# Weight copies spread out, splits without a table, two units' scores moved

## The chip, the cores and the metric

The kernel runs on one core of one Trainium2 chip. The metric is the device time of one execution in microseconds (us); the time before is the median of three executions. Five engines work side by side, each through its own instructions in order: PE (matrix multiply), ACT (activations and copies), DVE (vector), POOL (GpSimd) and SP, which here only issues DMAs. An instruction that waits holds up everything behind it on its engine, on SP's queue too.

## The reference, cut to what matters

```python
scores = np.matmul(q, k.transpose(0, 1, 3, 2)) / np.sqrt(D)       # q, k, v: 8 x 8 heads x 576 x 64
mask   = (rel >= 0) & (rel < 64)                                  # rel = query position - key position
attn   = softmax(np.where(mask, scores, -1e9))
x      = np.matmul(attn, v).transpose(0, 2, 1, 3).reshape(4608, 512)
h      = x @ w_in                                                 # 512 x 2048
g      = h * np.tanh(np.log1p(np.exp(h)))                         # mish; h itself above 20
out    = g @ w_out                                                # 2048 x 512
```

## The kernel before

The 4608 tokens are cut into 12 chunks of 384. A *unit* is one chunk of one pair of heads; there are 48, four to a chunk. A unit's **scores** (L433, 24 small matmuls) go through the softmax on DVE and ACT (L463 and L467, six blocks of 128 x 128; L479, L480 and L487 normalise). The result is turned: DVE transposes blocks of 32 x 32 (L525), one DMA writes the tile to DRAM (`turned`, L535), four DMAs read it back in the other order (`pT`, L533). Then PE forms the unit's **values** (L546). So between a unit's scores and its values stand ACT, DVE and five DMAs on SP.

The feed-forward part works in f32 by splitting an operand into a rounded part and a remainder, with three products for one. It has 16 blocks f of the hidden width. For chunks 0 to 3, `ffn_in` (L579) fills one of two PSUM banks `h`, ACT applies mish from the bank (L609, which frees it), the result is split (L618 to L624), and `ffn_out` (L656) adds into three banks.

Chunks 4 to 11 are taken two at a time, in four super-blocks, and for them the first matrix product is done with 7 products in place of 8 on combinations of operands. For that, `combine(i)` (L851) prepares, while chunks 2 and 3 run, seven matrices for each of the eight pairs of blocks (i, i + 8): three are plain quarters of the weights, copied SBUF to DRAM (L858), four are made by two sums (L863) and four differences (L868) on DVE, rounded on ACT (L871), the remainder formed on DVE (L872), and written to the same DRAM tensor `wc` (L875). A combine works in three tiles `o`, which also hold chunk 0 and 1's outputs until they are stored (L665). In the super-blocks `fetch` (L1036) brings one matrix after another back into seven slots.

On the other side `rebuild` (L1006) forms the seven combinations of the activations: `blend` (L1003) adds and subtracts on DVE, `split` rounds on ACT (L995, the *snap*) and forms the remainder on DVE (L996), into tiles that held weights. A blend is followed by splits that read its result, so ACT and DVE wait for each other in turn. A super-block then runs eight rounds i of seven products (L1051); the two banks X and V are read out by ACT (L1059) and DVE (`settle`, L1064).

The order on every engine is made by a list scheduler (`Plan.order`): of the tasks that are ready by its own cost table it takes the one with the lowest rank. ACT holds one table of functions at a time. A task that names a table (`exp` for the softmax, `mish`) puts a table load (L1241) in front of itself when another is in place, and is ranked 150 later for it; a task that names none runs under either. Tasks of chunks 2 and 3 stand in nine groups: within a group are some `ffn_in` blocks, then values and scores of one or two units, then the `ffn_out` of the group before. Group g of chunk 2 and 3 carries the ranks 1000 + 10 * step.

Of the kernel before, what the change touches and what calls it, by code (L numbers as in the profile page):

```python
# [9 lines left out]
F32 = mybir.dt.float32  # L10
# [198 lines left out]
def tile_window_attn_mish_ffn(  # L209
# [641 lines left out]
    def combine(i, rank):  # L851

        plan.key = None
        d, db = combined[i]
        (fa, fab), (fb, fbb), (hs, hsb) = zip(o_ring.tiles, o_ring.bufs)
        pair = i, i + NS
        for f, half, at in ((i, 0, 0), (i, 1, 1), (i + NS, 1, 2)):
            add("SP", "move", lambda f=f, half=half, at=at: nc.sync.dma_start(  # L858
                d[:, at * WP:(at + 1) * WP].rearrange("p (a n) -> p a n", a=2), ws[f][0][:, :, half * HW:(half + 1) * HW].bitcast(F32)),
                reads=[wbufs[f][0]], writes=[db], rank=4000 + i, size=P * WP * 4, after=[sums[1]])  # L860
        x = None
        for f, t, tb in ((i, fa, fab), (i + NS, fb, fbb)):
            x = add("DVE", "sum5", lambda f=f, t=t: nc.vector.tensor_tensor(  # L863
                t, ws[f][0][:, 0, :].bitcast(F32), ws[f][0][:, 1, :].bitcast(F32), ALU.add),
                reads=[wbufs[f][0]], writes=[tb], rank=rank, after=[x] if x else [])
        for o, a, b, tb in ((fa[:, :HW], fb[:, :HW], fa[:, :HW], fab), (fb[:, :HW], fb[:, HW:], fb[:, :HW], fbb),
                            (fb[:, HW:], fb[:, HW:], fa[:, :HW], fbb), (fa[:, HW:], fa[:, HW:], fb[:, HW:], fab)):
            x = add("DVE", "sub2", lambda o=o, a=a, b=b: nc.vector.tensor_tensor(o, a, b, ALU.subtract),  # L868
                    writes=[tb], rank=rank, after=[x])
        for t, tb, at in ((fa, fab, 3), (fb, fbb, 5)):  # L870
            y = add("ACT", "hi5", lambda t=t: nc.scalar.copy(hs.bitcast(F32R), t), reads=[tb], writes=[hsb], rank=rank, after=[x])  # L871
            add("DVE", "sum5", lambda t=t: nc.vector.tensor_tensor(t.bitcast(F32R), t, hs, ALU.subtract),  # L872
                reads=[hsb], writes=[tb], rank=rank, after=[y])
            for part, u, ub in ((0, hs, hsb), (1, t, tb)):
                add("SP", "move", lambda u=u, at=at, part=part: nc.sync.dma_start(  # L875
                    d[:, at * WP:(at + 2) * WP].rearrange("p (q a n) -> p q a n", q=2, a=2)[:, :, part, :],
                    u.rearrange("p (q n) -> p q n", q=2)), reads=[ub], writes=[db], rank=rank, size=P * WP * 4)
# [5 lines left out]
            groups.append([(c, f + i) for i in range(size)])  # L883
            f += size
    first = 5
    COMBINE = {0: [0], 1: [1], 2: [2], 3: [3], 4: [4], 5: [5, 6], 6: [7]}
    runs = {}

    def run(g, kind, i):
        runs.setdefault(g, []).append((kind, i))  # L890
# [4 lines left out]
    for g in range(4):  # L895
        for i in range(2):
            run(first + g, "v", 16 + 2 * g + i)
            run(first + g, "s", 18 + 2 * g + i)

    class Part:  # L900
        def __init__(self, late, k):
# [18 lines left out]
    for g, steps in enumerate(groups):  # L920
        r = 1000 + 10 * step
        for c, f in steps:
            ffn_in(c, f, 1000 + 10 * step, True, False)
            step += 1
        if g == first - 1:
            raws = [(Part(raw_late[p // 2], p % 2), [joined(xbufs[0]) for _ in range(2)]) for p in range(NPAIR)]
        asked = {kind: [units[i] for k, i in sorted(runs.get(g, [])) if k == kind] for kind in "vs"}
        near, far = H[(hs[0] + 1) % 2], H[hs[0] % 2]
        double = len(asked["v"]) > 1 or len(asked["s"]) > 1
        for _, b in (near, far) if double else ():  # L930
            assert b.readers or not b.writers
        first_v, last_v = (asked["v"][:1], asked["v"][1:]) if g < first and double else (asked["v"], [])
        for n, u in enumerate(asked["v"]):
            u.o = (near, B[1])[n] if double else B[2]
            assert u.o[1].readers or not u.o[1].writers

        def pay(vs):
            for u in vs:
                values(u, r, True)
                refill_v(u.n)  # L940

        def trailing(n):
            for c, f in held[:n]:
                ffn_out(c, f, r + 15, True)
            del held[:n]

        apart = g >= first
        if apart:
            trailing(1)
        else:  # L950
            pay(first_v)
        for n, u in enumerate(asked["s"]):
            u.place = doubled(n, near, far) if double else whole(B[:2])
            scores(u, r, True)
            refill_qk(u.n)
        pay([] if apart else last_v)
        for u in asked["s"]:
            softmax(u, 1480 if g == len(groups) - 1 else r + 20, False)
        if apart:
            trailing(1)  # L960
            pay(asked["v"])
        for u in asked["v"]:
            x_parts(u, r + 15)
        for u in asked["s"]:
            turn_dma(u, 1480 if g == len(groups) - 1 else r + 20)
        trailing(len(held))
        held = list(steps)
        for i in COMBINE.get(g, ()):
            combine(i, r + 25)
# [15 lines left out]
    def operand(o, k):  # L985
        return ws[2 * o + k + 2][0].rearrange("p a n -> p (a n)")

    def raw(p, par):
        return raws[p][0][:, par].rearrange("p a j -> p (a j)")

    def split(o, par, second, rank):
        for k in range(2):
            p = k + 2 * second
            rb, wb = raws[p][1][par], wbufs[2 * o + k + 2][0]
            x = add("ACT", "snap", lambda k=k, p=p: nc.scalar.copy(operand(o, k)[:, :CH], raw(p, par)), reads=[rb], writes=[wb], rank=rank, table="mish")  # L995
            add("DVE", "comb", lambda k=k, p=p: nc.vector.tensor_tensor(  # L996
                operand(o, k)[:, CH:2 * CH], raw(p, par), operand(o, k)[:, :CH].bitcast(F32), ALU.subtract),
                reads=[rb], writes=[wb], rank=rank, after=[x])
# [93 lines left out]
    def recall(f, rank):  # L1092
        d, db = parked[f]
        back_at[0] += 1
        t, tb = backs[back_at[0] % 2] if back_at[0] % 4 < 2 else t_ring.take()
        add("SP", "move", lambda: nc.sync.dma_start(plain(t), d), reads=[db], writes=[tb], rank=rank, size=P * CH * 4)
        return t, tb

    def add_up(s, f, par, t, tb):
# [57 lines left out]
    for s in range(NSUP):  # L1157
        ss = SQ // 2 + s
        follow = units[base + NS * (s + 1):base + NS * (s + 2)]
        begun = units[base + NS * (s + 2):base + NS * (s + 2) + 2]  # L1160
        second = []
        for i in range(NS):
            r += 100
            plan.key = None
            product(0, r)
            p1 = keep(X, r - 260)
            product(1, r)
            c11 = settle(V, p1, r - 250)
            product(2, r)
            u2 = keep(X, r - 260)  # L1170
            product(3, r)
            product(4, r)
            u3 = keep(X, r - 260)
            c11 = mish(c11, r - 245, [u3[2]])
            c22 = mish(settle(V, u3, r - 250), r - 248)
            park(i + NS, *c22, r - 240)
            take(2, r)
            product(5, r)
            c21 = direct(X, r - 250)
            park(i, *c21, r - 240)  # L1180
            product(6, r)
            c12 = mish(settle(V, u2, r - 250), r - 246)
            take(2, r)
            if follow and i in (1, 3, 5):
                pair_run(follow[i - 1:i + 1], follow[i + 1:i + 3], B, r)
            take(len(queue), r)
            queue += add_up(ss, i, 0, *c11) + add_up(ss, i + NS, 0, *c12)
            queue[0].ready(r)
            queue[NTT].ready(r)
        r += 100  # L1190
        plan.key = None
        first = queue[:]
        del queue[:]
        seconds = []
        for i in range(NS):
            seconds += add_up(ss, i, 1, None, None) + add_up(ss, i + NS, 1, None, None)
        queue += [x for a, b in ((first, seconds), (first[3:], seconds[3:]), (seconds[6:], seconds[9:])) for x in a[:3] + b[:3]]
        take(18, r)
        if s == NSUP - 1:
            break  # L1200
        pair_run(follow[6:], begun, A, r)
        rebuild(r + 10)
        queue += seconds[12:]
        take(24, r)
# [84 lines left out]
```

## Time and profile before

| what | value |
|---|---|
| median of 3 executions | 898.85 us (897.71 to 899.69) |
| the profiled execution, its own time | 900.08 us |
| its span, first to last instruction | 898.3 us |
| PE busy | 877.4 us, 98% of the span |
| PE granted clock, mean | 0.992 of full speed |
| DVE, ACT, POOL busy | 435.4, 444.0, 259.9 us (48, 49, 29%) |
| DMA | 196.73 MB, 219 GB/s on average |

The span is the profiler's; the execution's own time is 1.8 us longer, and that execution is 1.2 us above the median. PE is nearly always busy, so what can be won or lost lies in its few idle stretches and in the stretches where its clock is granted at less than full. By time, chunks 0 and 1 run to about 180 us, chunks 2 and 3 (with the combines) from there to about 342 us, the four super-blocks from there to the end.

### The profile page before, as it was taken

The numbers are of one execution on the slowest core, as the hardware profiler recorded it, in microseconds if no ns is written. First come the engines' busy times: TensorE is split into PE (matmuls) and PEld (weight loads), VectorE is DVE, ScalarE is ACT, GpSimd is POOL, SyncE is SP. The second block draws the span as 40 slices with busy tenths as digits, with TensorE's granted clock in tenths as the row PEclk, the third lists the DMA queues.
The fourth block names the chain that finished last, engine by engine and source line by source line (L and its number), as shares of the span: only waits on it lengthen the run. The fifth ranks groups of instructions, "written<-read, shape, count | busy, mean of one in ns | idle before, by whom it ended". The sixth has DMA issues, their size and how long they took to land.

```text
span 898.3 us, 17666 instructions
## 1 busy us (share of the span) xinstructions
PE 877.4 (98%) x6317; PEld 778.1 (87%) x6317; DVE 435.4 (48%) x1198; ACT 444.0 (49%) x1148; POOL 259.9 (29%) x339
## 2 busy tenths in 40 slices
PE   8999999998899989999999999999999999999998
PEld 6889988888788878999888899888898888999987
DVE  7989976335767775333625234436144433111100
ACT  7937867554636574545724356625265631222300
POOL 1000000041243323122265221266212257222373
PEclk9999999999999999999999999999999999999999
DMA  8655423696758766899976799976699882666551
GB/s 289 225 182 177 161 85 120 195 345 209 237 167 277 230 190 224 267 295 287 282 246 189 223 295 287 286 246 202 214 290 291 250 265 71 211 203 196 150 159 44
DMA packets 117127, 196.73 MB, mean 219 GB/s; under 512 B 12208, under 2 KB 64176, under 8 KB 115376
## 3 DMA queue, kind: packets, MB, share of 16 engines
q1 hardware_dynamic: 116608, 195.12, 68.9%
q8 instruction: 50, 0.82, 0.4%
q10 hardware_dynamic: 432, 0.49, 0.2%
q14 instruction: 37, 0.30, 0.1%
HBM read 143.13 MB, written 52.43 MB: 218 GB/s over the span
## 4 chain that ended last, share of the span: by engine, by line
PE 80%; DVE 6%; ACT 5%; DMA 4%; SPq 3%; issue 2%; POOL 0%; ACTq 0%; DVEq 0%
PE h L1051 26%; PE acc L656 20%; PE at L656 18%; PE h L579 8%; DMA wc<-o 2%; SPq L858 2%; PE at L433 2%; PE h L546 1%; ACT pr L467 1%; PE at L546 1%; ACT L1241 1%; PE acc L433 1%; ACT wa L467 1%; DVE o L868 1%; DMA st<-w 1%
## 5 line engine op out<-in xcount | busy, mean ns | idle before, releaser
L656 PE MATMUL acc<-w,g 128*128 128x512 f32 x708 | 176.2, 394 | 0.0
L656 PEld LDWEIGHTS acc<-w,g 128*128 128x128 f32 x708 | 130.9, 188 | 27.5 <-issue 2.2
L1064 DVE TENSOR_TENSOR t<-h,t 128x384 f32<-128x384 f32 x96 | 53.4, 556 | 207.9 <-PE h L1051 146.9
L1051 PE MATMUL h<-w 128*128 128x384 f32 x768 | 142.9, 339 | 2.1 <-DVE t L1064 2.0
L1051 PEld LDWEIGHTS h<-w 128*128 128x128 f32 x768 | 134.7, 188 | 8.2 <-DVE t L1064 3.4
L656 PE MATMUL at<-w,g 128*128 128x512 f32 (+1 forms) x495 | 118.8, 391 | 0.8 <-DVE g L619 0.8
L1051 PE MATMUL h<-w,late 128*128 128x384 f32 x576 | 112.4, 338 | 0.0
L1059 ACT COPY t<-h 128x384 f32<-128x384 f32 x96 | 45.8, 477 | 134.0 <-PE h L1051 130.9
L656 PEld LDWEIGHTS at<-w,g 128*128 128x128 f32 x495 | 92.2, 188 | 20.4 <-DVE g L619 1.2
L1051 PEld LDWEIGHTS h<-w,late 128*128 128x128 f32 x576 | 101.9, 189 | 5.1 <-ACT t L1059 2.2
L1082 POOL TENSOR_SCALAR g<-t 128x384 fp32r<-128x384 f32 x58 | 30.1, 519 | 192.0 <-ACT t L1069 118.7
L1241 ACT ACT_TABLE_LOAD x61 | 78.3, 1283 | 1.0
L656 PE MATMUL acc<-w,late 128*128 128x512 f32 x306 | 78.5, 397 | 0.0
L579 PE MATMUL h<-late,w 128*128 128x384 f32 x384 | 72.9, 343 | 3.9 <-ACT t L609 3.9
L467 ACT ACTIVATE pr<-pr,mx 128x128 f32<-128x128 f32 x186 | 72.7, 394 | 5.0 <-DVE mx L463 4.4
L579 PEld LDWEIGHTS h<-late,w 128*128 128x128 f32 x384 | 68.4, 192 | 6.4 <-ACT t L609 5.4
L1069 ACT ACTIVATE t<-t 128x384 f32<-128x384 f32 x96 | 49.6, 525 | 41.1 <-DVE t L1064 41.0
L579 PE MATMUL h<-xh,w 128*128 128x384 f32 x256 | 68.1, 336 | 0.0
L656 PEld LDWEIGHTS acc<-w,late 128*128 128x128 f32 x306 | 57.1, 189 | 11.3 <-issue 0.9
L1084 POOL TENSOR_TENSOR g<-t,g 128x384 fp32r<-128x384 f32 x58 | 60.2, 1038 | 4.3
L1082 POOL TENSOR_SCALAR late<-t 128x384 fp32r<-128x384 f32 x38 | 20.4, 538 | 122.7 <-ACT t L1069 87.6
L656 PE MATMUL at<-w,late 128*128 128x512 f32 x225 | 54.0, 390 | 0.0
(124 smaller groups left out, 1214.8 us busy)
## 6 DMA issues: line engine op xcount, KB each, us to landing
w<-wc SPq DMA_DIRECT2D x128, 256.0 KB, 3.6
late<-wc SPq DMA_DIRECT2D x96, 256.0 KB, 3.7
qk<-qk SPq DMA_DIRECT2D x45, 416.0 KB, 5.0
v_t<-v SPq DMA_DIRECT2D x48, 384.0 KB, 4.2
pT<-turned SPq DMA_DIRECT2D x160, 96.0 KB, 3.4
st<-w SPq DMA_DIRECT2D x13, 1024.0 KB, 4.8
parked<-t SPq DMA_DIRECT2D x64, 192.0 KB, 3.1
turned<-pr SPq DMA_DIRECT2D x28, 384.0 KB, 3.7
```

What stands on the lines that cost most here:

```text
L433: nc.tensor.matmul(t[par * BLK:(par + 1) * BLK, col:col + P], u.q[0][rows, n * BLK:(n + 1) * BLK], u.k[0][rows, n * BLK:n * BLK + P], star ...
L467: return add("ACT", "exp", lambda: nc.scalar.activation(pr[:, j, :], pr[:, j, :], AF.Exp, bias=mx[:, j:j + 1], scale=-1.0, accum_out=sm[:, ...
L546: nc.tensor.matmul(o_ps[rows, n * BLK:(n + 1) * BLK], v_t[:, n, rows], pT[:, 2 * par:2 * par + 2, h * NM + m, :], start=True, stop=True)
L579: nc.tensor.matmul(h_ps[:, :CH], ws[f][0][:, part, cc * P:(cc + 1) * P], xx[:, cc, :], start=cc == 0 and i == 0, stop=cc == NPAIR - 1 and ...
L656: nc.tensor.matmul(bank[:, lo:hi], g[:, a, t * P:(t + 1) * P], ws[f][1][:, n, lo:hi], start=(begin or f == 0) and i == 0, stop=f == NF - 1 ...
L1051: nc.tensor.matmul(bank[0][:, :CH], w_[:, part * HW + k * P:part * HW + (k + 1) * P], x_[:, lo:lo + CH], start=begin and k == 0 and m == 0 ...
L1059: x = add("ACT", "snap", lambda: nc.scalar.copy(t, bank[0][:, :CH]), reads=[bank[1]], writes=[tb], rank=rank, table=table)
L1064: x = add("DVE", "comb", lambda: nc.vector.tensor_tensor(t, bank[0][:, :CH], t, ALU.add), reads=[bank[1]], writes=[tb], rank=rank, after=[x])
L1069: add("ACT", "mishs", lambda: nc.scalar.activation(t, t, AF.Mish), writes=[tb], rank=rank, table="mish", after=[x, *after])
L1082: x = add("POOL", "poolgh", lambda: nc.gpsimd.tensor_scalar(g[:, 0, :], plain(t), 1.0, 0.0, ALU.mult, ALU.add), reads=[tb], writes=[gb], r ...
L1084: add("POOL", "poolgl", lambda: nc.gpsimd.tensor_tensor(g[:, 1, :], plain(t), g[:, 0, :].bitcast(F32), ALU.subtract), reads=[tb], writes=[ ...
L1241: nc.scalar.preload_act_table_set(TABLES[t.load])
```

## The change

Four edits. (1) In `combine`, the three plain copies of a pair of blocks are queued behind the two sums of that pair and get the combine's own rank; before, all 24 copies had a rank of 4000 and more, were bound only to the end of chunk 1 and stood together there. The first combine moves from group 0 to group 1, the last two share group 6. (2) The snaps of `split` name no table. (3) The scores and softmax of the last two units that chunk 3 carried (24 and 25) move into round 0 of the first super-block; that block's pairs of units then come in rounds 0, 2, 4 and 6 instead of 1, 3 and 5. The special rank 1480 for them goes. (4) Reads of parked tiles (`recall`) are ranked 300 earlier.

```diff
@@ combine
-        for f, half, at in ((i, 0, 0), (i, 1, 1), (i + NS, 1, 2)):
-            add("SP", "move", lambda f=f, half=half, at=at: nc.sync.dma_start(
-                d[:, at * WP:(at + 1) * WP].rearrange("p (a n) -> p a n", a=2), ws[f][0][:, :, half * HW:(half + 1) * HW].bitcast(F32)),
-                reads=[wbufs[f][0]], writes=[db], rank=4000 + i, size=P * WP * 4, after=[sums[1]])
         x = None
         for f, t, tb in ((i, fa, fab), (i + NS, fb, fbb)):
             x = add("DVE", "sum5", lambda f=f, t=t: nc.vector.tensor_tensor(
                 t, ws[f][0][:, 0, :].bitcast(F32), ws[f][0][:, 1, :].bitcast(F32), ALU.add),
                 reads=[wbufs[f][0]], writes=[tb], rank=rank, after=[x] if x else [])
+        for f, half, at in ((i, 0, 0), (i, 1, 1), (i + NS, 1, 2)):
+            add("SP", "move", lambda f=f, half=half, at=at: nc.sync.dma_start(
+                d[:, at * WP:(at + 1) * WP].rearrange("p (a n) -> p a n", a=2), ws[f][0][:, :, half * HW:(half + 1) * HW].bitcast(F32)),
+                reads=[wbufs[f][0]], writes=[db], rank=rank + 1, size=P * WP * 4, after=[x])
...
-    COMBINE = {0: [0], 1: [1], 2: [2], 3: [3], 4: [4], 5: [5, 6], 6: [7]}
+    COMBINE = {1: [0], 2: [1], 3: [2], 4: [3], 5: [4, 5], 6: [6, 7]}
...
             run(first + g, "v", 16 + 2 * g + i)
-            run(first + g, "s", 18 + 2 * g + i)
+            if g < 3:
+                run(first + g, "s", 18 + 2 * g + i)
...
-            softmax(u, 1480 if g == len(groups) - 1 else r + 20, False)
+            softmax(u, r + 20, False)
...
-            turn_dma(u, 1480 if g == len(groups) - 1 else r + 20)
+            turn_dma(u, r + 20)
@@ split
-            x = add("ACT", "snap", lambda k=k, p=p: nc.scalar.copy(operand(o, k)[:, :CH], raw(p, par)), reads=[rb], writes=[wb], rank=rank, table="mish")
+            x = add("ACT", "snap", lambda k=k, p=p: nc.scalar.copy(operand(o, k)[:, :CH], raw(p, par)), reads=[rb], writes=[wb], rank=rank)
@@ recall
-        add("SP", "move", lambda: nc.sync.dma_start(plain(t), d), reads=[db], writes=[tb], rank=rank, size=P * CH * 4)
+        add("SP", "move", lambda: nc.sync.dma_start(plain(t), d), reads=[db], writes=[tb], rank=rank - 300, size=P * CH * 4)
@@ rounds of a super-block
-            if follow and i in (1, 3, 5):
+            if follow and s == 0 and i % 2 == 0:
+                pair_run(follow[max(0, i - 2):i], follow[i:i + 2], B, r)
+            if follow and s and i in (1, 3, 5):
                 pair_run(follow[i - 1:i + 1], follow[i + 1:i + 3], B, r)
```

What this does to the order is shown at three places. The lines of the changed kernel lie 1 to 3 higher than those of the kernel before (L863 is its plain copy, L859 its sum, L996 its snap, L1004 its blend).

**Place 1: SP behind the end of chunk 1.** `turned_111` and `pT_64` belong to unit 12, `turned_112` and `pT_65` to unit 13; `wc<-w` are plain copies, `wc<-o` combined matrices. Before, from the middle of the 24 copies on:

```order
L858 DMA wc_135<-w 128x2x256 x3
L858 DMA wc_136<-w 128x2x256
L393 DMA qk_93<-qk 128x832
L535 DMA turned_111<-pr_96 128x768
L858 DMA wc_136<-w 128x2x256 x2
L858 DMA wc_137<-w 128x2x256 x3
L858 DMA wc_138<-w 128x2x256 x2
L533 DMA pT_64<-turned_111 32x4x192 x4
L535 DMA turned_112<-wa_118 128x768
```

The same stretch in the changed kernel:

```order
L665 DMA out<-o_116 128x512 x3
L863 DMA wc_131<-w 128x2x256 x3
L393 DMA qk_92<-qk 128x832
L875 DMA wc_131<-o_116 128x2x256 x3
L393 DMA qk_93<-qk 128x832
L535 DMA turned_111<-pr_96 128x768
L875 DMA wc_131<-o_116 128x2x256
L533 DMA pT_64<-turned_111 32x4x192 x4
L535 DMA turned_112<-wa_118 128x768
```

Between unit 12's `turned` and its four reads stood seven plain copies; now one combined matrix stands there, and the first combine's seven writes stand in front of all.

**Place 2: SP and DVE before unit 15's values.** `turned_111` and `pT_65` are unit 15's, `turned_112` and `pT_64` unit 16's; on DVE `sm_101` and `wa_118` are unit 15's, `sm_102` and `pr_96` unit 16's. SP before:

```order
L535 DMA turned_111<-pr_97 128x768
L535 DMA turned_112<-wa_118 128x768
L533 DMA pT_65<-turned_111 32x4x192 x3
L875 DMA wc_133<-o_116 128x2x256 x2
L533 DMA pT_65<-turned_111 32x4x192
```

SP in the changed kernel:

```order
L535 DMA turned_111<-pr_97 128x768
L863 DMA wc_134<-w 128x2x256 x3
L535 DMA turned_112<-wa_118 128x768
L533 DMA pT_65<-turned_111 32x4x192 x4
L875 DMA wc_134<-o_116 128x2x256
```

DVE in the changed kernel in the same stretch:

```order
L872 TENSOR_TENSOR o_116<-o_116 128x512
L566 TENSOR_TENSOR late<-at_127,late 128x384
L859 TENSOR_TENSOR o_116<-w 128x512
L479 TENSOR_SCALAR sm_101<-sm_101 128x6
L480 RECIPROCAL sm_101<-sm_101 128x6
L487 TENSOR_TENSOR wa_118<-wa_118,sm_101 128x768
L525 STREAM_TRANSPOSE pr_97<-wa_118 128x6x4x32
L479 TENSOR_SCALAR sm_102<-sm_102 128x6
L480 RECIPROCAL sm_102<-sm_102 128x6
L859 TENSOR_TENSOR o_116<-w 128x512
L487 TENSOR_TENSOR pr_96<-pr_96,sm_102 128x768
```

On SP the two combined writes that stood among unit 15's reads are gone, and three plain copies, which wait for the second sum on DVE (the lower L859), now stand ahead of unit 16's `turned` and of the reads. On DVE, unit 15's transposition follows its normalising directly; before, a sum stood between.

**Place 3: ACT and DVE in group 7 of chunk 3.** `sm2_103` is the softmax of unit 23; `w_939`, `w_1114`, `w_1016`, `w_1319` are operands that a snap writes; `t0_104<-h1_130` is the mish that frees a bank of `ffn_in`. ACT before:

```order
L557 COPY late_3201<-at1_127 128x2x192
L467 ACTIVATE wa1_118,sm2_103<-wa1_118,mx2_100 128x128 x2
L1241 ACT_TABLE_LOAD
L995 CAST w_939<-late_3201 128x384
L995 CAST w_1114<-late_3201 128x384
L1241 ACT_TABLE_LOAD
L467 ACTIVATE wa1_118,sm2_103<-wa1_118,mx2_100 128x128
L871 CAST o0_116<-o0_116 128x512
L467 ACTIVATE wa1_118,sm2_103<-wa1_118,mx2_100 128x128 x2
L1241 ACT_TABLE_LOAD
L995 CAST w_1016<-late_2771 128x384
L609 ACTIVATE t0_104<-h1_130 128x384
```

ACT in the changed kernel:

```order
L557 COPY late_3184<-at1_127 128x2x192
L467 ACTIVATE wa1_118,sm2_103<-wa1_118,mx2_100 128x128 x2
L996 CAST w_939<-late_3184 128x384
L467 ACTIVATE wa1_118,sm2_103<-wa1_118,mx2_100 128x128 x3
L996 CAST w_1114<-late_3184 128x384
L871 CAST o0_116<-o0_116 128x512
L996 CAST w_1016<-late_2750 128x384
L996 CAST w_1319<-late_2750 128x384
L1244 ACT_TABLE_LOAD
L609 ACTIVATE t0_104<-h1_130 128x384
```

DVE in the changed kernel in the same stretch:

```order
L525 STREAM_TRANSPOSE pr0_96<-pr1_97 128x6x4x32
L1004 TENSOR_TENSOR late_2750<-late_2750,late_3184 128x384
L479 TENSOR_SCALAR sm2_103<-sm2_103 128x6
L480 RECIPROCAL sm2_103<-sm2_103 128x6
L997 TENSOR_TENSOR w_939<-late_3184,w_939 128x384
L487 TENSOR_TENSOR wa1_118<-wa1_118,sm2_103 128x768
L1004 TENSOR_TENSOR late_2750<-late_2750 128x384
```

On ACT two of the three table loads are gone, and the snaps of `w_1016` and `w_1319` now both stand ahead of the mish. `w_1016` reads the result of the second blend on DVE, and that blend now stands behind unit 23's normalising.

## Rows read from the trace of the kernel before

**Rows 1.** Timeline of PE: start, duration, instruction, [idle before it <-what ended it].
```profile
204.68 1.22 PE L546 MATMUL at<-pT,v_t 128*64 128x64 f32 x24 [4.22 <-DMA turned<-wa]
...
243.12 1.55 PE L546 MATMUL at<-pT,v_t 128*64 128x64 f32 x24 [2.58 <-DMA pT<-turned]
...
324.66 5.97 PE L579 MATMUL h<-late,w 128*128 128x384 f32 x24 [2.77 <-ACT t L609]
...
347.50 1.49 PE L1051 MATMUL h<-w 128*128 128x384 f32 x6 [2.03 <-DVE t L1064]
```

**Rows 2.** Stretches: length, PE busy (instructions), granted clock, DMA share, GB/s.
```profile
0.00:60.00 60.00, 54.73 (x662) 1.00 0.69 234
...
205.00:209.00 4.00, 4.00 (x50) 0.57 0.98 285
243.00:247.00 4.00, 3.88 (x52) 0.62 0.74 207
325.00:329.00 4.00, 4.00 (x16) 0.63 0.61 179
348.00:352.00 4.00, 4.00 (x15) 0.57 1.02 321
```

**Rows 3.** PE's waits in the first 60 us: total, times, longest.
```profile
PE acc L433 <- DVE mx L463: 1.1, 1, 1.1
```

**Rows 4.** Timeline of SP, 193 to 220 us: start, duration of the issues, count.
```profile
193.15 0.63 SPq L535 DMA_DIRECT2D turned<-pr  x1
193.83 5.80 SPq L858 DMA_DIRECT2D wc<-w  x7
199.68 2.48 SPq L533 DMA_DIRECT2D pT<-turned  x4
...
214.90 0.34 SPq L535 DMA_DIRECT2D turned<-pr  x1
...
217.28 1.77 SPq L533 DMA_DIRECT2D pT<-turned  x4
```

**Rows 5.** Timelines of DVE and ACT, 182 to 191 us.
```profile
182.21 0.69 DVE L863 TENSOR_TENSOR o<-w 128x512 f32<-128x512 f32 x1 [1.80 <-DMA out<-o]
...
189.59 0.98 DVE L525 STREAM_TRANSPOSE pr<-wa 128x768 f32<-128x768 f32 x1
...
184.41 1.28 ACT L1241 ACT_TABLE_LOAD   x1
```

**Rows 6.** Groups by line and shape, 178 to 345 us: busy us, mean ns.
```profile
L868 DVE TENSOR_TENSOR o<-o 128x256 f32<-128x256 f32 x32 | 17.3, 541 | 0.6
...
L487 DVE TENSOR_TENSOR pr<-pr,sm 128x768 f32<-128x768 f32 x9 | 9.8, 1093 | 0.1
...
L871 ACT CAST o<-o 128x512 fp32r<-128x512 f32 x16 | 9.9, 617 | 20.5 <-DVE o L868 9.1 <-issue 6.0 <-DMA wc<-o 5.3
```

**Rows 7.** Timeline of SP, 234 to 244 us.
```profile
234.35 0.33 SPq L535 DMA_DIRECT2D turned<-pr  x1
237.15 0.33 SPq L535 DMA_DIRECT2D turned<-wa  x1
...
240.64 3.03 SPq L533 DMA_DIRECT2D pT<-turned  x5
```

**Rows 8.** Timeline of ACT, 322 to 325 us.
```profile
322.41 1.28 ACT L1241 ACT_TABLE_LOAD   x1
...
324.12 0.48 ACT L609 ACTIVATE t<-h 128x384 f32<-128x384 f32 x1
```

**Rows 9.** Timelines of DVE and POOL, 341 to 349 us.
```profile
341.10 4.08 DVE L996 TENSOR_TENSOR w<-late,w 128x384 fp32r<-128x384 f32 x4
...
347.37 1.00 DVE L996 TENSOR_TENSOR w<-late,w 128x384 fp32r<-128x384 f32 x2
...
341.50 1.19 POOL L624 TENSOR_TENSOR g<-t,g 128x384 fp32r<-128x384 f32 x1
```

**Rows 10.** DMA issues, 360 to 460 us: count, KB each, median us to landing.
```profile
w<-wc SPq DMA_DIRECT2D x28, 256.0 KB, 4.1
```

## The prediction

> **What bounds the kernel now.** I read the page first: PE is busy for 877.4 of 898.3 us, so at most 20.9 us of its idle time can go, and any edit that only makes another engine faster is worth nothing unless PE was waiting for that engine. Then I asked for PE's timeline and kept the idle stretches of two microseconds and more. There are four, and all lie between the end of chunk 1 and the first round of the super-blocks [rows 1]: 4.22 us before unit 12's values, 2.58 before unit 15's values, 2.77 in chunk 3 before an `ffn_in` that waits for ACT's mish to free its bank, and 2.03 in the first super-block's round 0, where DVE's settle is late. Together 11.6 us. The rest of the 20.9 stands at the start and the end of the program, which the change doesn't touch. Third, the granted clock by stretch: in the four microseconds after each pause it was 0.57, 0.62, 0.63 and 0.57 [rows 2], a mixture of the two levels 1.2 and 2.4 GHz. What that costs is 4 x (1 - clock): 1.7, 1.5, 1.5 and 1.7, together 6.4 us. A pause of 1.1 us in the first 60 us [rows 3] stands in a stretch whose clock is 1.00 [rows 2], so I take it that a pause well under 2 us leaves the clock alone; between 1.1 and 2.03 nothing here decides. All four pauses with their clock are thus worth 18.0 us, and that is the most the change can win.
>
> **The change part by part.**
>
> *Copies spread out, first pause.* Unit 12's `turned` was issued at 193.15, then SP spent 5.80 us on seven plain copies, and the four reads went out from 199.68 to 202.16 [rows 4]; PE started 2.5 us after that. PE had come for the data at 204.68 - 4.22 = 200.5. Now one combined matrix stands there (place 1). But the softmax of unit 12 comes later than before, because a combine stands in front of it: the first sum starts at 182.21 as before [rows 5], then comes a second one (0.69) and four differences of 0.54 [rows 6], which ends at 185.8; the rounding on ACT takes 0.62 [rows 6], so the softmax's table load starts at 186.4 and not at 184.41 [rows 5], 2.0 later. On DVE a sum and one block of unit 13 are put between the normalising and the transposition, 1.0 more. The transposition that ended at 190.6 [rows 5] ends at 193.6, so `turned` goes out only 0.5 later than it did; the copies had held it anyway. A read can follow its `turned` after 2.4 us (214.90 to 217.28 [rows 4]): 196.0. Four reads take 1.8 to 2.5 us [rows 4]: 198.2. PE starts 2.5 later, at 200.7, 0.2 after it asks. I leave 0.3 of the 4.22 (bounds 0 and 2, the latter if the sum has to wait for a combined matrix to land): -3.9, and -1.7 for the clock.
>
> *Copies spread out, second pause.* Unit 15's `turned` went out at 234.35, its last read at 240.64 [rows 7], PE started 2.5 later; it had asked at 240.5. In the new order (place 2) no sum stands before the transposition any more, so `turned` is 0.7 earlier, at 233.7 (bounds 0 and 1.7 earlier). Behind it come three plain copies, which wait for a sum on DVE, then unit 16's `turned`, which followed after 2.8 us [rows 7] and has one difference more in front (0.54): 237.0. Then the reads follow without the two combined writes, four at about 0.45 (217.28, 1.77 for four [rows 4]): the fourth at 238.7, PE at 241.2. That is 0.7 of the 2.58: -1.9, and -1.5 for the clock. Bounds: nothing gained (the copies wait long for their sum) and all of it. What waits behind the three copies on SP are unit 16's `turned` and both units' reads, and behind those PE.
>
> *No table for the snaps, third pause.* The mish that PE waits for began at 324.12, behind a table load at 322.41 and a snap [rows 8]. Two of three loads go (place 3), 2 x 1.28 = 2.6 us, and the rounding (0.62) and a snap (0.5) stand behind unit 23's last exponential instead of before it: it ends near 322.4 - 2.6 - 0.6 - 0.5 = 318.7. That would remove the pause. But the next snap, `w_1016`, needs the second blend, and the new order puts that behind unit 23's normalising on DVE: about 0.4 for sum and reciprocal (an estimate), 0.50 for a remainder [rows 9], 1.09 for the normalising [rows 6], 0.5 for the blend, with hand-overs 321.3. Two snaps and the load follow, 0.9 + 1.28, and the mish starts at 323.5, 0.6 earlier than before. So a wait for DVE takes the place of the loads. I leave 2.2 of the 2.77: -0.6, and the clock falls as before. Bounds 0 and -2.8.
>
> *Two units out of chunk 3, fourth pause.* On ACT, twelve exponentials and two loads stood before the snaps of the rebuild; on DVE, two normalisings and two transpositions (about 1.0 each) were mixed with it, and settle came last. They go to round 0, where ACT and DVE have the eight rounds' slack. What comes in their place is the last combine: 2 sums, 4 differences, 2 remainders, some 5 us of DVE, but ahead of unit 22's values, so that it fills time in which DVE waited. Settle was 2.03 late, and one transposition with its normalising alone is worth that. I leave 0.2 (bounds 0 and 2.03): -1.8 and -1.7.
>
> The slow part that remains there is this: four remainders took 4.08 us at 341.10, while POOL split an operand, and two took 1.00 at 347.37 [rows 9], so 1.02 against 0.50 each. On this the Trainium skill (SBUF — State Buffer, "Who interferes with whom") says that a DVE instruction with two inputs in SBUF and a GpSimd instruction reading SBUF exclude each other for the length of an instruction; the doubling in the rows agrees with it. By that rule every operation of a combine, moved beside POOL, could take twice as long, which is the first rival below.
>
> *What is added.* The moved scores cost PE the same time elsewhere. Round 0 gets a new neighbour: product 0 of round 1 follows the scores at once and needs their bank, so it may wait for DVE's second block: +0.3 (0 to 1). In chunk 3's first group a rounding that waits for four differences now precedes the second mish: +0.3 (0 to 1.5). The first super-block carries eight units' transfers and not six, but a fetch lands after 4.1 us [rows 10] and is asked for seven products ahead: 0, hidden by those products. The reads of parked tiles: 0; they stand among unit 30's and 31's reads, whose cover is the end of the block.
>
> **The sum**, against the profiled execution's 900.08: -3.9 - 1.7 - 1.9 - 1.5 - 0.6 - 1.8 - 1.7 + 0.6 = -12.5, so 887.6. That execution is 1.2 above the median of 898.85; against the median I say 886.4.
>
> **The rivals.**
> 1. One of the two smaller closings fails. Either the fourth pause stays (the last combine and the rebuild meet POOL on DVE, each operation at 1.02 and not 0.50: ten of them before settle are 5 us more): 886.4 + 3.5 = 889.9; or the second stays (copies held by their sum): 886.4 + 3.4 = 889.8. For it: the rows of 341 us. Against: the chain before both is shorter. With both, 893.3.
> 2. All four close, because the second blend comes earlier than I think: 898.85 - 18.0 = 880.9. Against it is the order on DVE.
> 3. The edit doesn't do what it says: PE's first wait only changes its name, since the sums hold SP as the copies did, and only the fourth pause closes: 898.85 - 2.9 = 896.
> 4. Slower: three plain copies per combine, each waiting for a sum that waits for an earlier matrix to land, block SP in every group, and the reads of all value groups come late. It decides from the point where the reads land over 3 us later than now. Price: a pause like the second with its clock, 4.1 us, in six groups, 24.6, plus the third and fourth as now (8.0), less the 18.0 of today: +15, about 913; with four groups late, +6, 905. For it: SP takes its queue in order, and the second sum is behind unit 15's normalising. Against: the plain copies cost SP 0.8 us each now and are spread thinly.
>
> **How the numbers follow.** Forecast 0.48; rival 1 0.27 (both closings failing 0.05 of it); rival 2 0.10; rival 3 0.08; rival 4 0.07. The range from 881.5 to 893.5 leaves out rival 4, most of rival 3 and a part of rival 2. From one measurement to no change about 0.2% can be told, 1.8 us. Faster by more than that: forecast, rivals 1 and 2 and half of rival 3: 0.89; within: 0.04; slower: 0.07.
>
> **What would show it.** In the new profile: PE's idle before L546 near 200 and 237 us under 1 us each, and the clock at 1.00 behind them; a pause of about 2 us before an L579 still ended by ACT's mish, with ACT waiting for the blend (L1004) ahead of it; no pause before L1052; about 60 table loads. It is wrong if PE waits for `turned` or `pT` in other groups, or if PE idles between 345 and 450 us.

## The result, and the profile after

The changed kernel takes 889.4 us, the median of three executions (888.21, 889.4 and 892.0); a fourth, of 949.78 at a mean clock of 0.852, is left out here and in the ratio (with it the median is 890.7). Beside the kernel before, run on the same chip, the ratio is 0.9894, 95% interval 0.9857 to 0.9931: about 9.5 us faster. The forecast of 886.4 was 3 us too low against 0.9894 x 898.85 = 889.3; the range held.

The profiled execution is the one of 892.0 us, the slowest of the three, span 890.2 (before 898.3), table loads 59 (before 61). First PE's idle stretches of over 1 us after the first 60 us, as in [rows 1] (start, duration, instruction, [idle before it <- what ended it]):

```profile
199.86 0.44 PE L579 MATMUL h<-xh,w 128*128 128x384 f32 x1 [1.48 <-ACT t L609]
...
235.78 0.45 PE L579 MATMUL h<-xh,w 128*128 128x384 f32 x1 [1.09 <-ACT t L609]
...
317.33 2.93 PE L579 MATMUL h<-late,w 128*128 128x384 f32 x8 [2.76 <-ACT t L609]
...
336.81 2.35 PE L1052 MATMUL h<-w 128*128 128x384 f32 x12 [1.64 <-ACT t L1060]
...
492.45 4.44 PE L1052 MATMUL h<-w 128*128 128x384 f32 x24 [1.06 <-ACT t L1075]
```

Then the granted clock behind them, as in [rows 2] (stretch: length, PE busy, clock, DMA share, GB/s):

```profile
0.00:60.00 60.00, 53.43 (x662) 1.00 0.71 234
200.00:204.00 4.00, 4.00 (x61) 1.00 0.82 274
236.00:240.00 4.00, 4.00 (x61) 1.00 0.85 231
317.00:321.00 4.00, 3.67 (x13) 0.59 0.93 260
337.00:341.00 4.00, 4.00 (x23) 1.00 0.48 129
492.00:496.00 4.00, 3.55 (x20) 1.00 0.66 208
```

No pause is ended by a DMA any more: all five are ended by ACT. The waits for `pT` are gone, but at each pause ACT itself was late. Before the first one (timelines of DVE and POOL, then ACT, then SP):

```profile
183.81 3.37 DVE L868 TENSOR_TENSOR o<-o 128x256 f32<-128x256 f32 x4
183.33 1.31 POOL L624 TENSOR_TENSOR late<-t,late 128x384 fp32r<-128x384 f32 x1
...
187.22 0.63 ACT L871 CAST o<-o 128x512 fp32r<-128x512 f32 x1 [2.87 <-DVE o L868]
187.86 1.28 ACT L1244 ACT_TABLE_LOAD   x1
...
198.03 1.28 ACT L1244 ACT_TABLE_LOAD   x1
199.32 0.87 ACT L609 ACTIVATE t<-h 128x384 f32<-128x384 f32 x2
...
197.75 1.74 SPq L533 DMA_DIRECT2D pT<-turned  x4
```

The four differences stand ahead of unit 12's maxima on DVE, the rounding ahead of its exponentials, and the mish that PE waits for comes last, behind unit 13's exponentials too. The other four on ACT's timeline:

```profile
234.72 0.62 ACT L871 CAST o<-o 128x512 fp32r<-128x512 f32 x1 [3.61 <-DVE o L868]
235.24 0.86 ACT L609 ACTIVATE t<-h 128x384 f32<-128x384 f32 x2
...
313.10 0.62 ACT L871 CAST o<-o 128x512 fp32r<-128x512 f32 x1 [1.39 <-DMA wc<-o]
314.55 0.93 ACT L996 CAST w<-late 128x384 fp32r<-128x384 f32 x2 [0.83 <-DVE late L1004]
315.50 1.28 ACT L1244 ACT_TABLE_LOAD   x1
316.79 0.87 ACT L609 ACTIVATE t<-h 128x384 f32<-128x384 f32 x2
...
335.39 0.98 ACT L996 CAST w<-late 128x384 fp32r<-128x384 f32 x2 [3.61 <-DVE late L1004]
336.28 0.47 ACT L1060 COPY t<-h 128x384 f32<-128x384 f32 x1
...
491.91 0.49 ACT L1075 ACTIVATE t<-h 128x384 f32<-128x384 f32 x1 [6.21 <-DMA parked<-t]
```

Four of the five have one pattern: a rounding or a snap has waited at the head of ACT's queue for DVE or for a store, and behind it stands a mish or a copy for which PE's data is already there. The fifth is another case: there the mish itself waits, by the profile for a store.

The account of the two profiled executions: pauses 11.6 to 6.97 us, the new one +1.06, one of 0.52 at 281 us gone: -4.1. Clock, as 4 x (1 - clock): 6.4 to 1.6, -4.8. In the first 60 us, where both kernels hold the same instructions, PE is busy 1.3 us less [rows 2], +1.3; this start differs from execution to execution (53.43 to 56.26 us busy in the fourteen profiles), and here it is the slowest of all. Together -7.6 of the 8.1 by which the spans differ. In this pair more of the gain is clock than idle time.

### The profile page after: what moved, and what is told of

It reads as the page before. It is cut to its first block, busy times and chain, and to the rows that moved or that the text cites. A ratio compares the mean times of both kernels' runs of the same rounds, so it can differ in the third digit from the quotient of the medians.

```text
span 890.2 us, 17684 instructions
## 1 busy us (share of the span) xinstructions
PE 871.9 (98%) x6317; PEld 772.2 (87%) x6317; DVE 439.4 (49%) x1198; ACT 439.2 (49%) x1146; POOL 262.5 (29%) x339
## 4 chain that ended last, share of the span: by engine, by line
PE 84%; DVE 6%; DMA 5%; ACT 3%; issue 1%; SPq 0%; POOL 0%; ACTq 0%; DVEq 0%
PE h L1052 27%; PE acc L656 23%; PE at L656 17%; PE h L579 10%; PE at L433 2%; PE h L546 2%; DMA wc<-o 1%; ACT pr L467 1%; PE at L546 1%; DMA parked<-t 1%; DMA st<-w 1%; PE acc L433 1%; DVE o L868 1%; DVE pr L463 1%; PE acc L546 1%
## 5 line engine op out<-in xcount | busy, mean ns | idle before, releaser
L1052 PE MATMUL h<-w 128*128 128x384 f32 x768 | 142.8, 339 | 2.8 <-ACT t L1060 1.6
L1052 PEld LDWEIGHTS h<-w 128*128 128x128 f32 x768 | 134.5, 188 | 9.2 <-ACT t L1060 4.5
L1052 PE MATMUL h<-w,late 128*128 128x384 f32 x576 | 111.5, 337 | 0.0
L1052 PEld LDWEIGHTS h<-w,late 128*128 128x128 f32 x576 | 101.0, 188 | 5.5 <-ACT t L1060 2.6
```

Source lines behind the costliest of these rows:

```text
L1052: nc.tensor.matmul(bank[0][:, :CH], w_[:, part * HW + k * P:part * HW + (k + 1) * P], x_[:, lo:lo + CH], start=begin and k == 0 and m == 0 ...
```

## The experiments

All ratios are to the kernel before, run on the same chip. **Theory A**: the gain is the first edit's, through the two early pauses. **Theory C**, formed on the first four runs: what is left is the order on ACT. In kernels with added orders L610 is the mish, L875 the rounding, L871 the differences, L1001 the snap, L1012 the blend, L1061 the product, L1069 its copy.

**One edit at a time.** The first alone (the first to third pieces of the diff on the kernel before):

```diff
-    COMBINE = {0: [0], 1: [1], 2: [2], 3: [3], 4: [4], 5: [5, 6], 6: [7]}
+    COMBINE = {1: [0], 2: [1], 3: [2], 4: [3], 5: [4, 5], 6: [6, 7]}
...
+                reads=[wbufs[f][0]], writes=[db], rank=rank + 1, size=P * WP * 4, after=[x])
```

> The kernel before with the first edit alone (copies spread, combinations one group later). Theory A: the gain is this edit's; the pauses near 200 and 237 us shrink to about 1.5 and 1.1 as in the changed kernel and the clock stays at 1.00 behind them: 2.7 + 1.7 + 1.5 + 1.5 = 7.4 us less. But the last combination now meets the rebuild and the exponentials of units 24 and 25, with three table loads more than before between 318 and 350 us; A gives back 2 to 5 us there, so the ratio is 0.994 to 0.998. Theory B (the pauses only change their names, and the gain lies at the end of chunk 3): both early pauses stay over 2 us, 1.000 or above.

Measured: 888.91 us, ratio 0.9892 (0.9874 to 0.991), as much as all four edits. The early pauses are 1.32 and 0.63 us. Table loads rise to 65 (64 expected), yet this is faster than Theory A has it: the late pauses cost less than I feared, in the profiled execution because the clock held. That can't be the whole reason, since the other three executions had a mean clock of 0.996 to 0.998, where this one had 1.000, and took as long (888.56 to 889.92 us). PE's timeline, then the stretches behind the late pauses:

```profile
315.77 4.43 PE L579 MATMUL h<-late,w 128*128 128x384 f32 x24 [1.92 <-ACT t L609]
...
336.31 2.37 PE L1051 MATMUL h<-w 128*128 128x384 f32 x12 [2.32 <-ACT t L1059]
```

```profile
316.00:320.00 4.00, 4.00 (x24) 1.00 0.94 280
337.00:341.00 4.00, 4.00 (x22) 1.00 0.95 281
```

The second alone:

```diff
-... rank=rank, table="mish")
+... rank=rank)
```

> The kernel before with the second edit alone (snaps ask for no table). Theory A: pause 3 before ffn_in stays, since the mish waits behind snaps that wait for DVE's second blend: at least 2 of its 2.77 us are left and the clock falls behind it; ratio 0.998 to 1.001. Theory B: the two table loads were that pause; it closes with its clock, 2.8 + 1.5 us, ratio 0.995.

Measured: 904.37 us, ratio 1.0067 (1.0044 to 1.0091), slower; neither theory said so. The profile shows two reasons. The first is the place of a load. In the kernel before, ACT loaded the table first and waited then (ACT before the `ffn_in` of 281 us, and the pause that was left):

```profile
276.23 1.28 ACT L1241 ACT_TABLE_LOAD   x1
...
280.49 0.59 ACT L662 COPY o<-acc 128x512 f32<-128x512 f32 x1 [2.45 <-DMA wc<-o]
280.97 0.88 ACT L609 ACTIVATE t<-h 128x384 f32<-128x384 f32 x2
...
281.52 4.44 PE L579 MATMUL h<-late,w 128*128 128x384 f32 x24 [0.52 <-ACT t L609]
```

With no table asked for, the load stands behind the wait and in front of the mish. ACT in that kernel, at 281 and at 327 us, then PE:

```profile
279.09 0.59 ACT L662 COPY o<-acc 128x512 f32<-128x512 f32 x1 [3.76 <-DVE wa L525]
279.70 1.28 ACT L1241 ACT_TABLE_LOAD   x1
...
323.99 0.62 ACT L871 CAST o<-o 128x512 fp32r<-128x512 f32 x1 [4.99 <-DVE o L868]
...
325.87 1.28 ACT L1241 ACT_TABLE_LOAD   x1
```

```profile
281.53 6.00 PE L579 MATMUL h<-late,w 128*128 128x384 f32 x24 [2.60 <-ACT t L609]
...
327.71 6.77 PE L579 MATMUL h<-late,w 128*128 128x384 f32 x24 [4.28 <-ACT t L609]
```

The load's 1.28 is most of the 2.1 by which the pause at 281 us grew. At 327 us a load stood in front of the mish before as well [rows 8]; there the second reason is the larger, a rounding that now waits 4.99 for its differences. Two loads fewer and two pauses longer, with the clock at 0.57 and 0.50 in the four microseconds from 281 and 327.

The third alone (the scores of units 24 and 25, the fourth to sixth pieces and the last of the diff):

> The kernel before with the third edit alone (scores of units 24 and 25 into the first block). Theory A: only the pause at 347.5 changes; it goes from 2.03 to 1.6 or less and the clock behind it stays at 1.00: 0.4 to 2.0 + 1.7 = 2.1 to 3.7 us, ratio 0.996 to 0.998. Theory B (the pause is DVE's own rebuild, not the units' work): it stays near 2.0, ratio 1.000.

Measured: 904.45 us, ratio 1.0064 (1.0042 to 1.0087). The pause at the rebuild fell to 1.30 with its clock kept, as Theory A has it; but PE waited 4.15, 1.32 and 3.39 us at 243, 284 and 327 us, and at 463 us, in the super-block, 1.99 and 0.70 for POOL's split of a parked tile. This profile is of the slowest of six executions (902.29 to 907.83 us), and why the pause at 243 us grew from 2.58 was not looked into. The changed kernel without the third edit:

> The changed kernel without its third edit (scores of units 24 and 25 stay in chunk 3). Theory A: the early pauses are those of the changed kernel (1.5 and 1.1, clock 1.00), but two units' exponentials and transpositions now stand in front of the rebuild beside the last combination: pause 4 is 3 us or more and the clock falls behind it, so 3 to 5 us slower than the changed kernel: ratio to the kernel before 0.993 to 0.996. Theory B: the third edit is worth nothing, 0.989 as the changed kernel.

Measured: 891.17 us, 0.9913 (0.9896 to 0.993). The early pauses are 1.21 and 0.63, a little under the expected; then 2.55 at 337 us with the clock at 0.73, where Theory A has 3 or more; but whether that is slower than the changed kernel the intervals don't tell. The changed kernel without the fourth edit (`rank=rank` for the parked tiles' reads):

> The changed kernel without its fourth edit (reads of parked tiles keep their old rank). Prediction: nothing, within 0.2% of the changed kernel, ratio 0.989, since no pause of over 1 us stands after 500 us in either kernel. Rival: reads among the last units' transfers come late for the split on POOL, a new pause after 700 us, 1 to 3 us more.

Measured: 892.78 us, 0.9933 (0.9919 to 0.9947). The rival's mechanism is there, though earlier than it said. PE and POOL:

```profile
449.84 0.73 PE L656 MATMUL at<-w,g 128*128 128x512 f32 x2 [1.99 <-POOL g L1083]
451.39 5.53 PE L656 MATMUL at<-w,g 128*128 128x512 f32 x16 [0.82 <-POOL g L1085]
...
447.72 0.51 POOL L1083 TENSOR_SCALAR late<-late 128x384 fp32r<-128x384 f32 x1 [2.04 <-PE acc L656]
...
449.27 1.11 POOL L1083 TENSOR_SCALAR g<-t 128x384 fp32r<-128x384 f32 x2
```

PE asks at 447.85, and the split that it needs (`g<-t`) starts at 449.27. Its tile's read was issued at 444.87, behind eight reads of `pT`; with the 3.9 us that the five such reads there took to land (median) it is in place at about 448.8. And in POOL's queue it stands behind a split that waited 2.04 us for PE to release its buffer. The changed kernel issues its first such read ahead of those of `pT` (442.90 against 443.31) and the others among them, splits that tile at 446.63, and has no such pause. So the fourth edit pays for what the third brings into that block: 2.8 us of idle time here. The same pause stood in the third edit's own run. The changed kernel without the second edit:

> The changed kernel without its second edit (the snaps ask for the mish table again). Theory E (the request made ACT load its table while it waited for DVE; without it the load of 1.28 us stands behind the wait and in front of the mish that PE waits for): the pause near 317 us goes from 2.76 to under 2.0 and its clock may stay, 0.8 to 2.5 us less than the changed kernel, ratio to the kernel before 0.986 to 0.989. Theory F (two loads less are time saved, as the prediction has it): 0.5 to 2.6 us more than the changed kernel, 0.990 or above.

Measured: 891.18 us, 0.9918 (0.9903 to 0.9932): undecided by time. The pause there was 1.93 and not 2.76 (at 315 us), as Theory E has it: the load lies before the wait, at 308.43, and the mish follows its rounding at once. But the clock fell behind it (0.61), and a pause of 2.02 at the rebuild with 0.67 came on top. Theory F's premise falls: this kernel has 59 table loads too, so in the new order the second edit saves none.

**The order on ACT.** Tasks are recorded in lists as they are added; the experiments only add dependencies, so no instruction is added or left out. First:

```diff
+    for x in [rounded[6][1], *snaps[4:14]]:
+        x.deps.add(mishes[3, 12])
```

> The changed kernel, order on ACT alone: the second rounding of combination 6 and the third and later pairs of snaps come behind the mish of ffn_in 12 of chunk 3. Theory C (each remaining pause is a rounding or snap that waits at the head of ACT's queue with a ready mish behind it): the pause of 2.76 near 317 us goes under 0.5, the clock behind it stays at 1.00 (was 0.59 over four us): 2.3 + 1.6 = 3.9 us less than the changed kernel, ratio to the kernel before 0.985. Theory D (DVE beside POOL is too slow there whatever the order): the pause moves behind the delayed snaps, the first products of the super-block wait 2 us or more, ratio 0.989.

Measured: 887.21 us, 0.9853 (0.9833 to 0.9874). The pause at 317 us is gone; but the one at the rebuild grew, as Theory D has it, and took the clock with it (2.50, still ended by the copy; 0.57 from 330 us). By these pauses alone 1.8 us were won (2.76 + 1.6 less 0.86 and 1.7). Another 1.7 lie in three pauses that this order doesn't touch (1.48 to 1.32, 1.09 to 0.61, 1.06 to none): in the other variants the second of them is as short and the third gone, so the profiled execution of the changed kernel was a poor one there. Second:

```diff
+    for x in snaps[12:14]:
+        x.deps.add(kept[0][0])       # the first product's copy
+    for x in blends[6:8]:
+        x.deps.add(kept[0][1])       # its settle
```

> The changed kernel, with the last blend and the last two snaps of the first rebuild behind the first product's copy and sum. Theory C: the pause of 1.64 before the third product (near 337 us) goes under 0.3; its clock was 1.00 already, so 1.4 us less than the changed kernel, ratio 0.988. Theory D: the pause stays, or returns at the last product of the round, which reads those snaps; ratio 0.989 to 0.991.

Measured: 886.51 us, 0.9856 (0.9836 to 0.9876). The pause fell only to 1.17, as another snap still stood ahead of the copy; time came from elsewhere, since the pause of 2.95 at 315 us, unchanged in cause, left the clock at 1.00. Both theories' ratios are missed. Third:

```diff
+    cut[0].deps.update(d for e in units[12].exps for x in e for d in x.deps if d.engine == "DVE")
+    rounded[0][0].deps.update(x for e in units[12].exps for x in e)
+    rounded[0][1].deps.add(mishes[2, 3])
+    rounded[3][0].deps.add(mishes[2, 13])
```

> The changed kernel, with the first combination's differences behind unit 12's maxima, its roundings behind unit 12's exponentials and the mish of ffn_in 3, and one later rounding (combination 3) behind the mish of ffn_in 13 of chunk 2. Theory C: the pauses of 1.48 (200 us) and 1.09 (236 us) go under 0.3 each, no clock to win: 2.2 us less than the changed kernel, ratio 0.987. Theory D (the tables and DVE set these, not the rounding): both stay, ratio 0.989. Bound against both: the later combinations are late for their buffer and the plain copies, a new wait of 1 to 2 us.

Measured: 887.66 us, 0.9866 (0.9847 to 0.9885). The pause at 200 us is gone, so the differences and the rounding were its cause. That at 236 changed its kind: 1.13 us for `pT`. The bound against both theories has a new wait of this size, but for another reason; why these reads are late was not followed up. All orders together:

> All three orders together on the changed kernel. Theory C: the sum, 3.9 + 1.4 + 2.2 = 7.5 us less than the changed kernel, ratio to the kernel before 0.981. Theory D: no more than 2 us less, 0.987 or above.

Measured: 883.43 us, 0.9816 (0.9794 to 0.9839), Theory C's 0.981. Left were 1.13 for `pT` at 233 us and 2.60 at the rebuild. Then with `snaps[10:14]` in place of `snaps[12:14]`:

> All orders together, with two more snaps (of the sixth operand) behind the first product's copy. Theory C: the pause of 2.60 near 328 us, which there ended with a copy behind a snap that waited 2.18 us for the third blend, goes to 0.7 or less and its clock (1.7) stays: 3 to 3.6 us less than with all orders, ratio to the kernel before 0.978. Theory D (DVE's rebuild is the bound): the pause moves to the product that reads these snaps, 0.981.

Measured: 882.95 us, 0.9841 (0.9821 to 0.9861): no gain, Theory C's number missed. The pause at the rebuild stayed at 2.49. ACT before it:

```profile
325.35 0.63 ACT L875 CAST o<-o 128x512 fp32r<-128x512 f32 x1 [2.63 <-DMA wc<-o]
...
327.67 0.51 ACT L1001 CAST w<-late 128x384 fp32r<-128x384 f32 x1 [1.29 <-DVE late L1012]
328.09 0.47 ACT L1069 COPY t<-h 128x384 f32<-128x384 f32 x1
```

I had moved the wrong snaps: the last combination's rounding waits for a store and the next snap for a blend. So that combination went behind the first settle:

```diff
+    cut[7].deps.add(kept[0][1])
```

> The same, with the last combination's differences, roundings and remainders behind the first round's settle on DVE. Theory C: DVE is free for the blends some 4 us earlier, no pause over 0.5 us between 310 and 345 us: 0 to 0.7 us less than without it, ratio 0.977. Rival: the last combination holds the three output tiles that chunk 3's evacuation needs, and PE waits for a bank between 330 and 350 us, 1 to 3 us more, 0.979 to 0.981.

Measured: 879.55 us (878.95 to 880.67), 0.9788 (0.9772 to 0.9805). This version beats both kernels, by 2.1% the one before and, by the quotient of the two ratios (0.9788 / 0.9894), by about 1.1% the changed one; the two were not run beside each other, but their intervals don't meet. From 305 to 345 us PE never stops (the changed kernel first, then this one):

```profile
305.00:345.00 40.00, 35.60 (x241) 0.96 0.75 241
```

```profile
305.00:345.00 40.00, 40.00 (x285) 1.00 0.78 246
```

## Why the prediction was right, and where it was wrong

The direction was right, and so was the main mechanism: the first edit alone gives the whole gain, most of it in the two early pauses and their clock. The clock came out as forecast: the three pauses that fell under 2 us kept 1.00, the one that stayed fell to 0.59. Of the signs, `no pause before L1052` failed (1.64 and 1.06), and the idle time near 200 and 237 us moved from L546 to an `ffn_in`. The terms:

- **First pause**, -3.9 and -1.7: measured -2.7 and -1.7. The reads did come in time. What failed is the step "ends at 185.8; the rounding on ACT takes 0.62 ..., so the softmax's table load starts at 186.4": I took 0.54 for a difference, from the mean of [rows 6], which mixes two cases: beside POOL's splits it was 3.37 / 4 = 0.84, away from them 1.80 / 4 = 0.45 (at 321.42 below), and the load came at 187.86. And I followed only unit 12 to its values, not the mish behind it. The third experiment on the order shows this cause. The reads were in time only because PE was late: the last went out at 199.49, so by my 2.5 us PE could start at 202.0; it did at 202.15, after the 1.48 that it lost to the mish.
- **Second pause**, -1.9 and -1.5, with +0.3 for a rounding ahead of a mish: measured -1.5 and -1.5. The added term was the whole pause that remained (1.09 of my bound of 1.5), only in chunk 2's last group and not in chunk 3's first; in the five variants of the changed kernel that leave this stretch alone it is 0.61 to 0.63. The 0.7 for the reads is not seen beside it, but with the mish out of the way the third order shows 1.13 for `pT`.
- **Third pause**, -0.6, clock falls: measured 0.0 and 0.59. The mechanism is the forecast one: the loads went, and the wait for the blend that I named took their place, with the last load behind it, where the sum has it. Mis-sized is the term "about 0.4 for sum and reciprocal (an estimate)": the first of the two took 0.99 and ended with POOL's split, the second 0.19. So the mish starts 2.2 after PE has come (316.79 against 314.57), not 1.6 as in the sum. The wait of a rounding for the store of its own tile (1.39) was not in the sum, but it ended first: the snap behind it still waited 0.83 for the blend. DVE of the changed kernel, then POOL:

```profile
311.52 0.99 DVE L479 TENSOR_SCALAR sm<-sm 128x6 f32<-128x6 f32 x1
...
311.08 1.40 POOL L624 TENSOR_TENSOR g<-t,g 128x384 fp32r<-128x384 f32 x1
```

- **Fourth pause**, -1.8 and -1.7: measured -0.4 and -1.7. Here half of the first rival came true, the rebuild that meets POOL: three remainders took 2.92 and two blends 1.84, 0.97 and 0.92 each, where a blend without POOL took 0.55, and the copy of the first product stood behind two snaps that waited 3.61 for them. The last combine did not meet POOL: its four differences took 1.80. DVE of the changed kernel, then a split on POOL:

```profile
321.42 1.80 DVE L868 TENSOR_TENSOR o<-o 128x256 f32<-128x256 f32 x4
...
329.75 0.55 DVE L1004 TENSOR_TENSOR late<-late 128x384 f32<-128x384 f32 x1
...
331.15 2.92 DVE L997 TENSOR_TENSOR w<-late,w 128x384 fp32r<-128x384 f32 x3
334.00 1.84 DVE L1004 TENSOR_TENSOR late<-late 128x384 f32<-128x384 f32 x2
...
331.69 1.19 POOL L624 TENSOR_TENSOR g<-t,g 128x384 fp32r<-128x384 f32 x1
```

  The Trainium skill (SBUF — State Buffer, "Who interferes with whom") lets a DVE instruction with two inputs in SBUF and a GpSimd one that reads SBUF exclude each other; the trace agrees in so far as these operations took up to twice as long. That the result, 889.3, lies near that rival's 889.9 is luck: the rival takes its 3.5 from this pause with its clock, and here only 1.4 was lost, with the clock kept. Of the 4.9 us between the sum's -12.5 and the account's -7.6, the fourth pause has 1.4, the first 1.2, the third 0.6, the second 0.4, and the start of the two executions 1.3.
- **Parked tiles**, 0: right for the sum, wrong in reason; without the fourth edit two pauses of 2.8 us together stand at 450 us.
- Not in the sum: 1.06 at the second super-block's start, and the 0.52 that left.

Of the rivals, the second (880.9) is what the last version reaches with 879.55, though by an added order and not by an earlier blend. The third (896) and the fourth (905 and more) lie outside the interval, whose upper end is 0.9931 x 898.85 = 892.6; but the third has a point, since the wait did change its name, to a shorter one. That the first edit brings the gain is shown by it alone (0.9892); which of its two parts does, the spread copies or the combines one group later, was not tried. That the second to fourth add nothing measurable on top of it holds within some 0.4%, the width of these intervals; alone the second and the third each cost 0.6 to 0.7%, and the fourth alone was not run.

## What to carry to other kernels

When an edit takes a wait from an in-order engine, list what now stands between each producer and the consumer that the bounding engine waits for; here four of the five pauses that were left were a ready instruction behind one that was not. Before you count a table load as saved, see whether it lay inside a wait: moved behind the wait, it stands in front of the instruction that needs it (1.28 of the 2.1 us at 281). And don't take a cost from a mean over two cases: the scheduler's table has one number for a difference (0.36), where the trace has 0.45 away from POOL's splits and 0.84 beside them. Correct the order, or the table, where the trace contradicts it.

## What was not expected of the hardware

A pause's length alone doesn't decide whether the granted clock falls. Over the fourteen profiles, between 190 and 500 us, pauses up to 1.81 us left it at 1.00 and those of 3.39 and more brought it down. In between both happened: of twenty pauses, those of 1.92, 2.32, 2.49 and 2.95 us left it at 1.00, while the other sixteen, from 1.93 to 2.90, brought it to 0.56 to 0.73 in the four microseconds from there. Two rows, 2.95 before 315 us in the second order and 1.93 in the kernel without the second edit:

```profile
316.00:320.00 4.00, 4.00 (x24) 1.00 0.88 262
```

```profile
315.00:319.00 4.00, 3.80 (x14) 0.61 0.98 298
```

What else decides was not tried. The executions of one kernel seem to differ in this: of the kernel with the pause of 2.49 (two more snaps behind the copy), three took 882.38, 882.89 and 882.95 us at a mean clock of 1.000, and two 885.11 and 886.67 at 0.998 and 0.997. So the 1.6 us that go with such a pause are a matter of one execution as much as of the kernel, and the worth of a single pause should not be read closer than that from one profile.
